# Six chunk-0 loads of a fused RWKV and MLP kernel issued by ScalarE in place of SyncE

## The chip, the core and the metric

The kernel runs on one core of a Trainium2 chip. A core has TensorE (matmuls; it reads SBUF and writes PSUM), VectorE, ScalarE and GpSimd (work on tiles, each taking its own instructions in order) and SyncE, which here does nothing but issue DMAs. ScalarE issues some DMAs as well, between its other instructions. The profile calls the engines PE (and PEld for weight loads), DVE, ACT, POOL and SP; ACTq and SPq are the instruction queues in which an engine issues its DMAs. The metric is the device time of one execution in microseconds, from inputs in DRAM to the output in DRAM.

## The reference

Inputs are r, k and v of shape (4 batches, 8 heads, 768 steps, 48), decays w and bonuses u of shape (8, 48), and an MLP with gain g and weights 384 x 1536 and 1536 x 384, all in float32. A recurrence over the steps is followed by a normalised two-layer MLP with a residual:

```python
for t in range(S):
    kt, vt, rt = (k[:, :, t].copy(), v[:, :, t].copy(), r[:, :, t].copy())
    cur = np.einsum('bhd,bhe->bhde', u[None] * kt, vt)
    y[:, :, t] = np.einsum('bhd,bhde->bhe', rt, state + cur)
    state = w[None, :, :, None] * state + np.einsum('bhd,bhe->bhde', kt, vt)
...
xn = (x - mu) / np.sqrt(var + 1e-06) * g_ln
ch = np.maximum(xn @ w_ch1, 0.0) @ w_ch2
return (x + ch).astype(np.float32)
```

Here x is y with its 8 heads side by side, 384 wide.

## The kernel before

**Tiles.** The 768 steps are cut into 6 chunks of 128. A tile i is chunk i // 4 of batch i % 4, so there are 24 tiles, and tiles 0 to 3 are chunk 0 of the four batches. Within a chunk the recurrence becomes matrix products: r and k are scaled by powers of the decay (steps SR and SK, which write `sc`), transposed (TR on TensorE, copied to SBUF by TCr, TCk or TC), multiplied into a 128 x 128 matrix per head (AT) and masked (AM, AMa, AMb, on VectorE). Y multiplies that with v and adds the state of earlier chunks; S makes the next state and the bonus term, of which ZU and CC take the parts out of PSUM. Q is the product of the transposed r and k for the bonus, CV turns v to bf16, VB multiplies v by the bonus, and X adds it to Y. Then come the MLP's steps: XN (centre), LT and XT (transpose), UP and RL (first layer), DN (second layer), OT (scale and residual), STO (store).

**Pairs in chunk 0.** Batches 0 and 1 share one pair of tiles, and so do 2 and 3. A load of chunk 0 takes 192 KB of one batch to 64 partitions, two neighbouring steps in each; the tile that SK, SR and CV read is one of the two steps over all 128 partitions. So SK0 and SK1 each read what LK0 and LK1 loaded, SR2 and SR3 what LR2 and LR3 loaded, CV2 and CV3 what LV2 and LV3 loaded, and so on. From chunk 1 on a load fills a tile of its own.

**Order.** The order of all work is written out by hand in `PLAN`: each entry is a step's name, its index and a letter for the engine or the PSUM bank. Every engine takes its own entries in that order; between engines there are semaphores alone. The letter s stands for ScalarE, v for VectorE and g for GpSimd. The loads LK, LR and LV (lines 376 to 383) all call `load` (lines 363 to 371), which issues one DMA from SyncE and has no use for the letter, which in the plan is "-". SyncE issues a load as soon as it comes to it, unless the tile's ring slot is still in use or its queue is full. A helper `issuer(e)` (line 206) is used by the small loads at the start and by the stores: it gives ScalarE for s, and SyncE for anything else.

**Around the change.** The plan's entries for SyncE begin with LK1, LV0, LR1, LR0, LK0, LK2, LK3, LV1, LR2, LR3, LV2, LR4, LV3, LV4, LR5, LK4, LK5 and then the three LW1 (768 KB each of the first layer's weights). ScalarE's entries begin with four small loads (WF and three LC), the table load TL, the logarithm LN, and then the exponentials and copies GK0, CP, FK, GR1, GR0, GK1, FR (which overwrites LN's output in place), CV1, TCk0, UGC, TCr0, TCk1, WL, CC0, TCr3, TCk3, TCr2, CC1, CV3, VB0. TensorE's order is WB, CT, dummy matmuls DU, TR0, TR1, DU, AT0, TR3, S0, AT1, DU, TR2, S1, Y1, AT3, AT2, S3, Y0, TR4, and so on up to UP0. GpSimd's entries, after the constants, are SK0, UW, SR3, SR2, Q1, CV2, VB1, SK4, SR4, Q2, SK5. VectorE's are SR1, SR0, SK1, SK3, SK2, CV0, TCr1, Q0 and the masks.

Of the kernel before, what the change touches and what calls it, by code (L numbers as in the profile page):

```python
# [15 lines left out]
K_BY_DMA = [12, 13, 14, 15, 16, 17, 18, 19, 20, 21, 22, 23]  # L16
SLOTS = {'kf': 10, 'rf': 10, 'vf': 11, 'sc': 5, 'vv': 5, 'trs': 5, 'q': 3, 'A': 4, 'cc': 5, 'Z': 6, 'ZS': 2, 'Vb': 4, 'x': 12, 'xn': 6, 'xT': 4, 'hT': 4, 'ot': 4}
PLAN = """
MZ,0,g MI,0,g MM,0,g WF,0,s MW,0,v LC,0,s LC,2,s LC,1,s WB,0,h LK,1,- LV,0,- LR,1,- LR,0,- TL,0,s LN,0,s MP,0,v MQ,0,v LK,0,- GK,0,s SK,0,g CT,0,o
CP,0,s FK,0,s UW,0,g GR,1,s SR,1,v DU,39,h GR,0,s SR,0,v TR,0,- GK,1,s SK,1,v TR,1,o FR,0,s LK,2,- LK,3,- SK,3,v SK,2,v LV,1,- CV,1,s TCk,0,s UGC,0,s  # L20
CV,0,v TCr,1,v TCr,0,s LR,2,- LR,3,- DU,11,p Q,0,v AT,0,- AMa,0,v AMb,0,v SR,3,g TR,3,h TCk,1,s WL,0,s S,0,o CC,0,s ZU,0,v AT,1,- DU,2,a AMb,1,v
TCr,3,s TCk,3,s Q,3,v AMa,1,v SR,2,g TR,2,- TCr,2,s TCk,2,v Q,1,g S,1,h CC,1,s LV,2,- LR,4,- LV,3,- CV,2,g LV,4,- LR,5,- SR,5,v Y,1,h ZU,1,v AT,3,-
AM,3,v VB,1,g X,1,v AT,2,- CV,3,s S,3,- ZU,3,v VB,0,s Y,0,h X,0,v LK,4,- SK,4,g SR,4,g AMb,2,v AMa,2,v XN,1,s TR,4,h TC,4,s CV,4,s SQ,1,s CC,3,v Q,4,v
Q,2,g S,2,h ZU,2,v CC,2,v VB,2,v LT,1,- LK,5,- SK,5,g TR,5,h TC,5,v LW1,0,- SW,1,s SW,0,s Y,3,o XN,0,g LT,0,- XT,0,s XT,1,s SW,2,g VB,3,g Y,2,h X,2,v
X,3,v LW1,1,- SW,3,v SW,5,g Q,5,v S,4,- SW,4,s UP,0,- CC,4,s RL,0,s UP,16,- RL,16,s XN,2,g LT,2,o XT,2,v ZU,4,v LW1,2,- SW,8,s SW,7,g ATP,4,- AM,4,v
# [40 lines left out]
def kernel(  # L66
# [12 lines left out]
    nc = tc.nc  # L79
    P = nc.NUM_PARTITIONS  # L80
    B, H, S, D = r.shape
# [8 lines left out]
    FK = F // P  # L90
# [23 lines left out]
    def ring(name, shape, dtype):  # L114
        n = SLOTS[name]
        tiles = [const.tile(shape, dtype, name=f"{name}{a}") for a in range(n)]
        return lambda i: tiles[i % n]

    def pairs(name, shape, dtype):
        n = SLOTS[name]  # L120
        tiles = [const.tile([P, 2] + shape, dtype, name=f"{name}{a}") for a in range(n // 2)]
        rest = [const.tile([P] + shape, dtype, name=f"{name}_{a}") for a in range(n % 2)]
        return tiles, lambda i: tiles[i % n // 2][:, i % n % 2] if i % n // 2 < len(tiles) else rest[0][:]

    kp, kf = pairs("kf", [H, D], FP32)
    rp, rf = pairs("rf", [H, D], FP32)
    vp, vf = pairs("vf", [H, D], FP32)
# [78 lines left out]
    def issuer(e):  # L206
        return nc.scalar if e == "s" else nc.sync

    def chunk_src(t, i):
        c, b = divmod(i, B)  # L210
        return t[b, :, c * L : (c + 1) * L, :].rearrange("h t d -> t h d")
# [148 lines left out]
    def both(t, i):  # L360
        return t[i // 2][:].rearrange("p a h d -> p (a h d)").rearrange("p (h j d) -> p h j d", h=H, j=2)

    def load(ring, pair, src, i):
        if i >= B:
            nc.sync.dma_start(out=ring(i), in_=chunk_src(src, i))  # L365
        else:
            b0 = i % 2 * DP
            nc.sync.dma_start(  # L368
                out=pair[i // 2][b0 : b0 + DP].rearrange("p a h d -> p (a h d)").rearrange("p (h x) -> p h x", h=H),
                in_=src[i, :, :L, :].rearrange("h (p j) d -> p h (j d)", j=2),  # L370
            )
# [2 lines left out]
        return ring(i) if i >= B else both(pair, i)[:, :, i % 2]  # L374

    def LK(i, e):
        load(kf, kp, k, i)

    def LR(i, e):
        load(rf, rp, r, i)  # L380

    def LV(i, e):
        load(vf, vp, v, i)

    def SK(i, e):
        times(e, sck(i)[:, :, :D], rows_of(kf, kp, i), Fk[:] if i >= B else F0[i % 2][1][:])
# [316 lines left out]
    def STO(i, e):  # L703
# [11 lines left out]
        MQ=MQ, MZ=MZ, GK=GK, GR=GR,  # L715
        WF=WF, WB=WB, LC=LC, CT=CT, CP=CP, LT2=LT2, TKR=TKR, DU=DU, MW=MW, TL=TL, MI=MI, MM=MM, MP=MP, LN=LN, FK=FK_, FR=FR_, UGC=UGC,
        UW=UW, WL=WL, LW1=LW1, SW=SW, LW2=LW2, CW=CW, LK=LK, LR=LR, LV=LV, SK=SK, SR=SR, CV=CV, TR=TR, TCr=TCr,
        TCk=TCk, TC=TC, Q=Q, AT=AT, ATP=ATP, AMa=AMa, AMb=AMb, AM=AM, S=S_, CC=CC, ZU=ZU, ZD=ZD, VB=VB, Y=Y, X=X,
        SQ=SQ, XN=XN, RS=RS, LT=LT, LTD=LTD, TKD=TKD, TRD=TRD, XT=XT, UP=UP, RL=RL, DN=DN, OT=OT, STO=STO, DA=DA, DB=DB, OA=OA, OB=OB, SA=SA, SB=SB,
    )  # L720
    for step in PLAN.split():
        name, i, e = step.split(",")
# [31 lines left out]
```

## Time and profile before

| what | us |
|---|---|
| median of three runs | 153.09 |
| the three runs | 151.73 to 153.7 |
| the profiled execution | 153.01 |
| its span, first to last instruction | 151.2 |
| busy in the span: TensorE matmuls | 139.2 |
| VectorE | 113.4 |
| GpSimd | 88.2 |
| ScalarE | 86.4 |

The span is the part of an execution that the trace shows; the 1.8 us around it belong to the run's time. A row of a timeline gives the start of a group of like instructions, how long the group lasted, the engine, the line of the kernel, the operation and the tiles (written <- read); the bracket at its end is the time that the engine stood idle ahead of it and what ended that. Many steps share the line of a helper (204 for products, 199 and 201 for copies), so the tiles tell them apart: `sc<-rf` is an SR, `sc<-kf` an SK, `vv<-vf` a CV, `Vb<-vf,cc` a VB. DMA-issuing instructions are not counted as busy time. A load's landing is the time from its issue until its data is there.

### The profile page before, as it was taken

How to read it: one execution, taken by the hardware profiler on the slowest of the kernel's cores; microseconds unless marked ns; L12 is line 12 of the kernel's file. 1: busy time of each engine (PE TensorE's matmuls, PEld its weight loads, DVE VectorE, ACT ScalarE, POOL GpSimd, SP SyncE). 2: the span in 40 equal slices, each digit the busy share in tenths (PEclk: the TensorE clock that was granted, in tenths of full speed). 3: DMA queues.
4: the chain of work that ended last, by engine and by line, in shares of the span. 5: the costliest groups of instructions: out<-in, count | busy, mean ns of one | idle time of the engine just before them, and what ended most of it. 6: DMA issues, size and time to landing. Idle time of an engine off the chain costs nothing.

```text
span 151.2 us, 4597 instructions
## 1 busy us (share of the span) xinstructions
PE 139.2 (92%) x1843; PEld 112.2 (74%) x1843; DVE 113.4 (75%) x224; ACT 86.4 (57%) x228; POOL 88.2 (58%) x115
## 2 busy tenths in 40 slices
PE   3398959999999999998999979999999999999992
PEld 1247748999977779885679749977778966979781
DVE  3087997599978899699798897887974566866352
ACT  1667967586965526686328354688873640543710
POOL 7055699782999595787375682639615139741000
PEclk9999995699999999999999999999999999999999
DMA  2999999799988997999889999999999994850112
GB/s 62 237 225 195 179 336 353 142 181 327 377 167 177 216 181 152 201 225 182 169 124 237 203 168 188 206 174 243 175 255 215 251 153 90 231 154 5 56 52 104
DMA packets 92868, 28.61 MB, mean 189 GB/s; under 512 B 88364, under 2 KB 91056, under 8 KB 92848
## 3 DMA queue, kind: packets, MB, share of 16 engines
q1 hardware_dynamic: 91952, 27.24, 85.6%
q10 hardware_dynamic: 896, 1.09, 2.0%
q8 instruction: 14, 0.23, 0.6%
q14 instruction: 6, 0.05, 0.1%
HBM read 18.88 MB, written 4.72 MB: 156 GB/s over the span
## 4 chain that ended last, share of the span: by engine, by line
PE 65%; DMA 10%; SPq 10%; DVE 7%; issue 3%; POOL 2%; ACT 2%; DVEq 0%; ACTq 0%
PE hp L610 19%; PE o L640 12%; PE s L640 11%; DMA vf<-in_v_dram 7%; SPq L368 6%; PE o L610 4%; DMA kf<-in_k_dram 3%; PE at L435 3%; DVE A L445 3%; PE s L610 3%; SPq L365 2%; PE at L399 1%; PE hp L485 1%; PE hp L538 1%; PE hp L516 1%
## 5 line engine op out<-in xcount | busy, mean ns | idle before, releaser
L610 PEld LDWEIGHTS <-w_sb 128*128 128x128 bf16 x612 | 49.8, 115 | 3.1 <-issue 0.6
L610 PE MATMUL hp<-xT,w_sb 128*128 128x128 bf16 (+1 forms) x456 | 42.0, 242 | 0.4 <-DVE x L545 0.4
L640 PEld LDWEIGHTS <-hT 128*128 128x128 bf16 x276 | 24.9, 98 | 15.0 <-ACT hT L626 1.5
L626 ACT ACTIVATE hT<-hp 128x512 bf16<-128x512 f32 x40 | 23.5, 594 | 18.7 <-PE hp L610 17.0
L445 DVE TENSOR_TENSOR A<-at,mask 128x1024 bf16<-128x1024 f32 (+1 forms) x27 | 29.2, 1097 | 3.3 <-PE at L435 3.3
L640 PE MATMUL o<-w_sb,hT 128*128 128x384 bf16 x144 | 27.4, 326 | 1.2 <-ACT hT L626 1.0
L640 PE MATMUL s<-w_sb,hT 128*128 128x384 bf16 x132 | 25.4, 326 | 0.0
L204 POOL TENSOR_TENSOR q<-trs 128x512 bf16<-128x512 bf16 x11 | 13.1, 1202 | 10.9 <-DMA trs<-sc 4.1
L204 POOL TENSOR_TENSOR Vb<-vf,cc 128x384 f32<-128x384 f32 x14 | 11.9, 852 | 9.0 <-issue 4.2
L204 POOL TENSOR_TENSOR sc<-rf,Fr 128x384 bf16<-128x384 f32 x13 | 13.6, 1045 | 5.1 <-DMA rf<-in_r_dram 5.1
L204 POOL TENSOR_TENSOR sc<-kf,Fk 128x384 bf16<-128x384 f32 x14 | 14.6, 1048 | 2.7 <-DMA kf<-in_k_dram 2.1
L552 ACT ACTIVATE sqj<-x,sm 128x384 bf16<-128x384 f32 x24 | 14.7, 611 | 0.1
L545 DVE SCALAR_TENSOR_TENSOR x<-hp,Vb 128x384 f32<-128x384 f32 x20 | 10.9, 551 | 4.9 <-PE hp L538 2.6
L628 DVE TENSOR_SCALAR hT<-hp 128x512 bf16<-128x512 f32 x12 | 8.3, 688 | 7.8 <-PE hp L610 7.7
L199 ACT CAST vv<-vf 128x384 bf16<-128x384 f32 x11 | 5.5, 508 | 11.0 <-DMA vf<-in_v_dram 11.0
L560 POOL TENSOR_SCALAR xn<-x,sm 128x384 bf16<-128x384 f32 x12 | 7.3, 611 | 7.5 <-DVE x L545 7.3
L204 POOL TENSOR_TENSOR Z<-ZS,WLZ 128x384 bf16<-128x384 f32 x9 | 9.0, 1013 | 1.2 <-DVE ZS L498 1.2
L201 POOL CAST vv<-vf 128x384 bf16<-128x384 f32 x10 | 6.0, 603 | 5.3 <-DMA vf<-in_v_dram 4.8
L610 PE MATMUL o<-xT,w_sb 128*128 128x256 bf16 (+1 forms) x84 | 9.1, 250 | 0.0
L698 DVE SCALAR_TENSOR_TENSOR ot<-o,rs,x 128x384 f32<-128x384 f32 x12 | 7.3, 611 | 1.7 <-PE o L640 1.1
L399 PEld LDWEIGHTS <-sc 128*128 128x128 bf16 x96 | 6.7, 108 | 2.1 <-POOL sc L204 1.8
L698 DVE SCALAR_TENSOR_TENSOR ot<-s,rs,x 128x384 f32<-128x384 f32 x11 | 6.7, 611 | 1.5 <-PE s L640 1.5
(138 smaller groups left out, 236.9 us busy)
## 6 DMA issues: line engine op xcount, KB each, us to landing
kf<-in_k_dram SPq DMA_DIRECT2D x24, 192.0 KB, 3.9
vf<-in_v_dram SPq DMA_DIRECT2D x24, 192.0 KB, 4.1
rf<-in_r_dram SPq DMA_DIRECT2D x24, 192.0 KB, 4.1
w_f<-in_moe_w_ch_dram SPq DMA_DIRECT2D x6, 768.0 KB, 6.1
out_dram<-ot SPq DMA_DIRECT2D x18, 192.0 KB, 3.4
out_dram<-ot ACTq DMA_DIRECT2D x5, 192.0 KB, 1.9
trs<-sc SPq DMA_TRANSPOSE x12, 3.4
xT<-xn SPq DMA_TRANSPOSE x9, 3.8
```

The costliest lines, as they stand in the source:

```text
L204: engines[e].tensor_tensor(out=out, in0=in0, in1=in1, op=ALU.mult)
L368: nc.sync.dma_start(out=pair[i // 2][b0 : b0 + DP].rearrange("p a h d -> p (a h d)").rearrange("p (h x) -> p h x", h=H), in_=src[i, :, :L, ...
L399: nc.tensor.transpose(out=t[:, a * HP + q, :], in_=flat[:, q, :], identity=ident[:])
L445: nc.vector.tensor_tensor(out=AA(i)[:, a:b].rearrange("p e q t -> p (e q) t"), in0=psum["at", i][:, a:b].rearrange("p e q t -> p (e q) t") ...
L545: nc.vector.scalar_tensor_tensor(out=xx(i)[:], in0=psum["y", i][:, :C], scalar=1.0, in1=Vb(i)[:], op0=ALU.mult, op1=ALU.add, accum_out=sm[ ...
L552: nc.scalar.activation(out=sqj[:], in_=xx(i)[:], func=ACT.Square, bias=sm[i][:], scale=-float(C), accum_out=sq[g][:, j : j + 1])
L560: engines[e].tensor_scalar(out=xn(i), in0=xx(i)[:], scalar1=-float(C), scalar2=sm[i][:], op0=ALU.mult, op1=ALU.add)
L610: nc.tensor.matmul(out=t[:, a * gw : (a + 1) * gw].rearrange("p (j t) -> p j t", j=size), lhsT=w1_sb[n][kc][:, fb::FB], rhs=xT(g)[:, :size ...
L626: nc.scalar.activation(out=o, in_=s, func=ACT.Relu)
L628: nc.vector.tensor_relu(out=o, in_=s)
L640: nc.tensor.matmul(out=psum["o", i][:, :C], lhsT=hT(g)[:, fk, j * P : (j + 1) * P], rhs=w2_sb[d][:, a, :], start=(seen == 0 and a == 0), s ...
L698: nc.vector.scalar_tensor_tensor(out=ot(i), in0=psum["o", i][:, :C], scalar=rs[g][:, j : j + 1], in1=xx(i)[:], op0=ALU.mult, op1=ALU.add,)
```

## The change

In chunk 0, the loads of k, r and v of the second batch (index 1) and of the fourth (index 3) get the letter s in the plan, at the places at which they stood. The load functions hand the letter on, and `load` uses `issuer(e)`. The six DMAs are the same; ScalarE issues them, each between the ScalarE entries around it: LK1 and LR1 between the small loads and TL, LK3 and LV1 between FR and CV1, LR3 between TCr0 and TCk1, LV3 between CC1 and CV3. Loads with "-" stay with SyncE, and all other entries stay as they were.

```diff
-MZ,0,g MI,0,g MM,0,g WF,0,s MW,0,v LC,0,s LC,2,s LC,1,s WB,0,h LK,1,- LV,0,- LR,1,- LR,0,- TL,0,s LN,0,s ...
+MZ,0,g MI,0,g MM,0,g WF,0,s MW,0,v LC,0,s LC,2,s LC,1,s WB,0,h LK,1,s LV,0,- LR,1,s LR,0,- TL,0,s LN,0,s ...
-... FR,0,s LK,2,- LK,3,- SK,3,v SK,2,v LV,1,- CV,1,s TCk,0,s UGC,0,s
+... FR,0,s LK,2,- LK,3,s SK,3,v SK,2,v LV,1,s CV,1,s TCk,0,s UGC,0,s
-CV,0,v TCr,1,v TCr,0,s LR,2,- LR,3,- DU,11,p Q,0,v ... TCk,1,s ...
+CV,0,v TCr,1,v TCr,0,s LR,2,- LR,3,s DU,11,p Q,0,v ... TCk,1,s ...
-... S,1,h CC,1,s LV,2,- LR,4,- LV,3,- CV,2,g LV,4,- LR,5,- ...
+... S,1,h CC,1,s LV,2,- LR,4,- LV,3,s CV,2,g LV,4,- LR,5,- ...

-    def load(ring, pair, src, i):
+    def load(ring, pair, src, i, e):
         if i >= B:
-            nc.sync.dma_start(out=ring(i), in_=chunk_src(src, i))
+            issuer(e).dma_start(out=ring(i), in_=chunk_src(src, i))
         else:
             b0 = i % 2 * DP
-            nc.sync.dma_start(
+            issuer(e).dma_start(
...
     def LK(i, e):
-        load(kf, kp, k, i)
+        load(kf, kp, k, i, e)
```

LR and LV hand on their letter in the same way.

More of the change, by code (lines that the diff above doesn't have):

```diff
@@ L18 @@
 PLAN = """
[L19 to L22, printed above, removed]
+MZ,0,g MI,0,g MM,0,g WF,0,s MW,0,v LC,0,s LC,2,s LC,1,s WB,0,h LK,1,s LV,0,- LR,1,s LR,0,- TL,0,s LN,0,s MP,0,v MQ,0,v LK,0,- GK,0,s SK,0,g CT,0,o
+CP,0,s FK,0,s UW,0,g GR,1,s SR,1,v DU,39,h GR,0,s SR,0,v TR,0,- GK,1,s SK,1,v TR,1,o FR,0,s LK,2,- LK,3,s SK,3,v SK,2,v LV,1,s CV,1,s TCk,0,s UGC,0,s
+CV,0,v TCr,1,v TCr,0,s LR,2,- LR,3,s DU,11,p Q,0,v AT,0,- AMa,0,v AMb,0,v SR,3,g TR,3,h TCk,1,s WL,0,s S,0,o CC,0,s ZU,0,v AT,1,- DU,2,a AMb,1,v
+TCr,3,s TCk,3,s Q,3,v AMa,1,v SR,2,g TR,2,- TCr,2,s TCk,2,v Q,1,g S,1,h CC,1,s LV,2,- LR,4,- LV,3,s CV,2,g LV,4,- LR,5,- SR,5,v Y,1,h ZU,1,v AT,3,-
 AM,3,v VB,1,g X,1,v AT,2,- CV,3,s S,3,- ZU,3,v VB,0,s Y,0,h X,0,v LK,4,- SK,4,g SR,4,g AMb,2,v AMa,2,v XN,1,s TR,4,h TC,4,s CV,4,s SQ,1,s CC,3,v Q,4,v
@@ L376, in LK @@
     def LK(i, e):
-        load(kf, kp, k, i)
+        load(kf, kp, k, i, e)
     def LR(i, e):
-        load(rf, rp, r, i)
+        load(rf, rp, r, i, e)
     def LV(i, e):
-        load(vf, vp, v, i)
+        load(vf, vp, v, i, e)
     def SK(i, e):
```

## The prediction

> **What bounds the kernel now.** I read the page first, then the stretches of the span, the chain of waits from its start, the timelines of SyncE, ScalarE, GpSimd and TensorE up to 30 us, and last the landing times of single loads. In the stretches, the columns are the busy time of each engine, the granted TensorE clock, the share of the DMA engines and what they moved.
>
> ```profile
> span 151.2 us, 4597 instructions
> 6.00:8.00 2.00, 1.62 (x5) 0.93 (x6) 0.00 (x0) 1.01 (x3) 0.00 (x0) 1.00 1.27 218
> 20.00:22.00 2.00, 0.62 (x8) 0.45 (x8) 2.00 (x7) 0.95 (x2) 2.00 (x2) 1.00 1.03 378
> 20.00:30.00 10.00, 8.50 (x138) 7.40 (x140) 7.29 (x21) 6.30 (x13) 8.72 (x11) 0.66 0.95 286
> 30.00:40.00 10.00, 10.00 (x202) 9.63 (x199) 9.40 (x19) 8.19 (x21) 6.64 (x7) 1.00 0.99 289
> 100.00:110.00 10.00, 9.81 (x119) 7.06 (x118) 8.29 (x17) 8.21 (x26) 7.48 (x8) 1.00 1.13 225
> ```
>
> There are two regimes. From 30 us TensorE is busy 10.00 of 10.00 us, and from 100 to 110 still 9.81, so it is the bound and has next to no gaps that could soak up a late start. Ahead of 30 us the kernel is a chain of dependent steps: TensorE works 0.62 of the 2 us from 20 to 22, and its clock is 0.66 in the mean from 20 to 30. A delay in the early chain is therefore paid in full at the end. The DMA engines are full early too (share 1.27 from 6 to 8 us, at 218 GB/s, by which one load of 192 KB takes 197 / 218 = 0.90 us).
>
> SyncE issues the loads one after another (start, duration, queue, line, tile):
>
> ```profile
> 0.73 0.77 SPq L368 DMA_DIRECT2D kf<-in_k_dram  x1
> 2.23 1.52 SPq L368 DMA_DIRECT2D rf<-in_r_dram  x2
> 3.79 1.99 SPq L368 DMA_DIRECT2D kf<-in_k_dram  x3
> 5.83 0.83 SPq L368 DMA_DIRECT2D vf<-in_v_dram  x1
> 6.70 1.75 SPq L368 DMA_DIRECT2D rf<-in_r_dram  x2
> 10.21 1.57 SPq L368 DMA_DIRECT2D vf<-in_v_dram  x1
> 14.08 4.84 DMA kf<-in_k_dram
> 18.99 0.67 POOL sc L204
> 27.62 2.16 PE hp L610 x24
> ```
>
> By the order of the plan, LK1 is at 0.73, LR1 is the first of the two at 2.23, LK3 is the last of the three at 3.79, LV1 is at 5.83, LR3 the second of the two at 6.70, LV3 at 10.21: all six are on their way by then, however late their users come. The last three rows are from the chain of waits: a K load of chunk 1 (4.84 us) releases GpSimd at 18.99, and from 27.62 on the chain is TensorE.
>
> **The six issues on ScalarE.** ScalarE takes its steps in order. Its timeline around the new places:
>
> ```profile
> 2.58 0.64 ACTq L222 DMA_DIRECT2D rows<-in_u_dram  x1
> 3.25 1.28 ACT L240 ACT_TABLE_LOAD   x1 [3.25 <-DVE eps L290]
> 6.99 0.17 ACT L199 COPY cols<-o 128x11 f32<-128x11 f32 x1 [1.30 <-PE o L229]
> 9.21 0.61 ACT L315 ACTIVATE Fr<-Fr,pow_i 128x384 f32<-128x384 f32 x1
> 11.19 0.51 ACT L199 CAST vv<-vf 128x384 bf16<-128x384 f32 x1 [1.36 <-DMA vf<-in_v_dram]
> 12.70 0.58 ACT L199 COPY trs<-at 128x512 bf16<-128x512 bf16 x1
> 17.10 0.17 ACT L199 COPY cc<-hp 128x8 f32<-128x8 f32 x1
> 17.29 0.51 ACT L199 CAST vv<-vf 128x384 bf16<-128x384 f32 x1
> 94.70 0.60 ACT L626 ACTIVATE hT<-hp 128x512 bf16<-128x512 f32 x1 [0.88 <-PE hp L610]
> 94.71 0.39 ACTq L712 DMA_DIRECT2D out_dram<-ot  x1
> 88.62 0.60 DVE L698 SCALAR_TENSOR_TENSOR ot<-s,rs,x 128x384 f32<-128x384 f32 x1
> ```
>
> The three rows at the foot say when a DMA on ScalarE goes out. The row at 88.62 is VectorE's last output product ahead of the store, so the store's data was there no later than 88.62 + 0.60, yet it was issued at 94.71, 0.01 us after the activation ahead of it had stopped waiting 0.88 us for TensorE. So an issue does not pass a waiting step, but it needn't wait for that step's end (94.70 + 0.60).
>
> The Trainium skill (Perfetto Trace Analysis, section "DVE / Act Engine Instruction") has the sequencer push an activation into a wait queue and then fetch the next instruction. Taken alone, that would let all six loads leave early, in about 153 us; the 94.71 row disagrees.
>
> *LK1 and LR1* come behind the small loads, ahead of the table load. Two issues at about 0.65 us (the 0.64 of the row at 2.58) move the table load from 3.25 to about 4.6, and the work behind it by 1.4 us; the copy at 6.99 had idled 1.30 us for TensorE, so only 0.15 us is left at the exponential at 9.21. LR1 leaves at about 4.0, not at 2.23. Its users:
>
> ```profile
> 8.20 1.06 DVE L204 TENSOR_TENSOR sc<-rf,F 128x384 bf16<-128x384 f32 x2 [3.79 <-ACT F L276]
> 10.69 0.53 PE L300 MATMUL hp<-warm 128*128 128x128 bf16 x3
> ```
>
> At 5.3 us from issue to landing (the 5.5 below is its nearest row when the queue is full) LR1 lands at 9.3, and VectorE's pair SR1, SR0 starts 1.1 us late, ending at 10.4. That lies beside the dummy matmuls, which keep TensorE until 10.69 + 0.53 = 11.2. I cost it at nothing; if LR1 landed after about 10 us the cover would be gone, at 1 us for each us.
>
> *LK3 and LV1* stand behind the exponential at 9.21: LK3 goes at 9.4, not about 5.1, LV1 at 10.05, not 5.83. Behind LV1 stands the cast CV1 at 11.19, which needs that load, and behind the cast the copies of the transposed tiles, the last at 12.70. For the landings I have these rows (the median from issue to landing of the loads issued in a short stretch, in us):
>
> ```profile
> kf<-in_k_dram SPq DMA_DIRECT2D x1, 192.0 KB, 3.2
> rf<-in_r_dram SPq DMA_DIRECT2D x2, 192.0 KB, 5.5
> rf<-in_r_dram SPq DMA_DIRECT2D x1, 192.0 KB, 5.9
> kf<-in_k_dram SPq DMA_DIRECT2D x1, 192.0 KB, 9.2
> rf<-in_r_dram SPq DMA_DIRECT2D x1, 192.0 KB, 4.2
> ```
>
> They were issued at 0.73 (empty engines), about 7.4, 9.34, about 19.9 (behind the weights) and 28.98. What a load on ScalarE's own queue takes while SyncE's is full, no row shows: 3.2 us is the low end, 5.9 the high end, 9.2 the end beside the weights. For LV1, second of two, I take 5.5, as issued nearest in time. It lands at 10.05 + 5.5 = 15.55 and CV1 starts 4.4 us late. VectorE is stuck as well: SK3 needs LK3, and CV0 reads the tile that LV0 and LV1 share.
>
> *LR3* stands behind the copy at 12.70, 1.5 us after the cast of which 0.5 was idling: 15.55 + 1.0 = 16.55. It used to be issued at 7.4. Landing 4.84 us, as the K load of 14.08, gives 21.4. Who waits for it:
>
> ```profile
> 13.06 2.14 POOL L204 TENSOR_TENSOR sc<-rf,F 128x384 bf16<-128x384 f32 x2 [1.88 <-DMA rf<-in_r_dram]
> 16.26 0.50 POOL L201 CAST vv<-vf 128x384 bf16<-128x384 f32 x1
> 17.35 0.83 POOL L204 TENSOR_TENSOR Vb<-vf,cc 128x384 f32<-128x384 f32 x1 [0.59 <-ACT cc L199]
> 18.99 1.00 POOL L204 TENSOR_TENSOR sc<-kf,Fk 128x384 bf16<-128x384 f32 x1 [0.81 <-DMA kf<-in_k_dram]
> 19.95 1.00 POOL L204 TENSOR_TENSOR sc<-rf,Fr 128x384 bf16<-128x384 f32 x1
> 14.12 0.62 PE L399 MATMUL hp<-ident,sc 128*128 128x128 bf16 x8 [0.37 <-POOL sc L204]
> 21.00 0.62 PE L399 MATMUL hp<-ident,sc 128*128 128x128 bf16 x8 [1.18 <-POOL sc L204]
> ```
>
> GpSimd's SR3 starts at 21.4 in place of 13.06, 8.3 us late. TensorE's TR3 (14.12) is queued ahead of S0, AT1, TR2 and S1, and ScalarE's copy CC1 at 17.10 follows S1, so all of it moves by 8.3 us; CC1 starts at 25.4.
>
> *LV3* stands behind CC1, is issued at 25.45 in place of 10.21, and with 4.2 us (the row of 28.98) lands at 29.65. Both casts CV2 (GpSimd, 16.26) and CV3 (ScalarE, 17.29) read the tile of which it is half. GpSimd now runs CV2 at 29.65, VB1 (0.83) at 30.15, SK4 at 31.0, SR4 at 31.9, without its old waits of 0.59 and 0.81. TR4, behind SR4, starts at 32.95 in place of 21.00.
>
> **The SyncE side.** Its queue loses six issues and every later load is issued up to some 5 us sooner: LK4, LK5 and the weights no longer are what ends last. That gain, the 0.81 us, is already in the sum, because TR4 is placed by GpSimd without that wait. SyncE has no new wait. The DMA engines move the same bytes.
>
> **The sum.** +4.4 by CV1, +3.9 more by SR3, +3.65 more by TR4, together 32.95 - 21.00 = 11.95 us. From TR4 on GpSimd, VectorE and TensorE follow in the same order. The low clock (0.66 from 20 to 30) comes after the idle stretch of TensorE, which both kernels have there, so I count no change for it. The profiled execution took 153.01 us (151.2 of span and 1.8 around it; the median of the runs is 153.09): 153.0 + 12.0 = 165.0 us.
>
> By the Trainium skill (DMA: Bandwidth & Descriptors, section "Queues, rings and completion order") each DMA engine takes turns between the queues. ScalarE's loads would then overtake SyncE's backlog: an estimate is 3.2 + 0.9 = 4.1 us for a single load, LV1 at 15.3, and about 163.9 us in all. No row here has two full queues.
>
> **The rivals.** *A smaller delay:* the new queue is served at once, each load 3.2 us. LV1 is 2.3 us earlier, LR3 1.6 more and LV3 1.0 more: 165.0 - 4.9 = 160.1; if LR3 is also issued as soon as CV1 has stopped waiting (16.55 becomes 15.7) 159.3. For it: ScalarE's queue is empty. Against it: the DMA share is at or above 1.0 throughout.
>
> *A larger one:* LR3 and LV3, issued when the weights are moving, take 5.9 to 9.2 us. 5.9 for all three adds 0.4 + 1.1 + 1.7 = 3.2, so 168.2; 9.2 for one of them adds some 4 more, 172. Against it: the weights were sent sooner, and LV3 may come after them.
>
> *Faster:* SyncE's serial issues are what bound the start. The six removed took some 5.5 us (0.77 + 0.76 + 0.66 + 0.83 + 0.87 + 1.57, means where a row holds several), so LK4 leaves at 8.6 and lands at 13.4 instead of 18.9. The idle 1.18 us of TensorE at 21.00 goes, and with it, if it caused the clock of 0.66, up to 10 x 0.34 = 3.4 us: 153.0 - 1.2 - 3.4 = 148.4. It decides only if LV1, LR3 and LV3 land by 11.2, 13.1 and 16.3, that is, if ScalarE's issues pass its waiting copies. The 94.71 row speaks against that. *No change* needs the same passing, with the first loads late by as much as SyncE's are early: about 153.
>
> **How the numbers follow.** Forecast (161 to 168) 0.68; smaller delay (156 to 161) 0.16; larger 0.08; no change 0.05; faster 0.03. The likeliest is 165.0. The range 159 to 169 goes from the low end of all three landings to just above their high end and leaves out some 0.17. About 2% is what a measurement of this kernel can tell from no change, 150.0 to 156.2: faster 0.03, within 0.05, slower 0.92.
>
> **What would show it.** ScalarE's table load near 4.6; its issues of LK3 and LV1 at 9.4 to 10.1, of LR3 just after CV1 (15 to 17), of LV3 behind CC1 (24 to 26). GpSimd idle for rf until about 21, then for vf until about 29.5; TensorE idle ahead of TR3; the chain's first UP group near 39.5 in place of 27.62. The forecast is wrong if ScalarE issues LR3 ahead of CV1's start, if its loads land within 3 us or need over 6, or if TensorE after 40 us has gaps that the late start fills.

## The result, and the profile after

| kernel | median, us | to the kernel before | 95% interval |
|---|---|---|---|
| before | 153.39 | | |
| changed | 170.19 | 1.110 | 1.098 to 1.123 |

The change costs 16.8 us, 11%. The direction and the path were as forecast; 165.0 was too low, and the time lies above the range. The profiled execution of the changed kernel took 168.47 us with a span of 166.7, so 15.5 us more span than before; the other three runs took 169.68 to 170.92. The medians here and below are over all runs; the ratios and their intervals leave out slow runs, those more than 1.5% above the fastest of the same kernel.

ScalarE's timeline of the changed kernel (start, duration, queue or engine, line, tiles; the bracket is the idle time ahead and what ended it):

```profile
4.69 1.28 ACT L240 ACT_TABLE_LOAD   x1 [4.69 <-DVE pow L258]
9.45 0.60 ACTq L368 DMA_DIRECT2D kf<-in_k_dram  x1
10.09 0.65 ACTq L368 DMA_DIRECT2D vf<-in_v_dram  x1
16.19 0.51 ACT L199 CAST vv<-vf 128x384 bf16<-128x384 f32 x1 [6.14 <-DMA kf<-in_k_dram]
16.30 0.67 ACTq L368 DMA_DIRECT2D rf<-in_r_dram  x1
30.87 0.17 ACT L199 COPY cc<-hp 128x8 f32<-128x8 f32 x1 [0.25 <-PE hp L485]
30.88 0.60 ACTq L368 DMA_DIRECT2D vf<-in_v_dram  x1
33.91 0.51 ACT L199 CAST vv<-vf 128x384 bf16<-128x384 f32 x1 [2.88 <-DMA vf<-in_v_dram]
```

Each late load goes out as soon as the last step ahead of it that had to wait has started: LK3 0.01 us after FR (9.44), LV1 right behind it at 10.09, LR3 0.11 us after the start of CV1 at 16.19, LV3 0.01 us after CC1 at 30.87. LR3 did not wait for the copies TCk0 and TCr0, which stand between CV1 and it in the plan and started at 16.61 and 17.20. The bracket at 16.19 names a K load, but what CV1 reads is v: by the trace, LV1 took 6.0 us to land, which is 16.1. GpSimd and TensorE wait for them in turn:

```profile
25.11 1.95 POOL L204 TENSOR_TENSOR sc<-rf,F 128x384 bf16<-128x384 f32 x2 [14.90 <-DMA rf<-in_r_dram]
33.95 0.50 POOL L201 CAST vv<-vf 128x384 bf16<-128x384 f32 x1 [5.78 <-DMA vf<-in_v_dram]
34.41 0.83 POOL L204 TENSOR_TENSOR Vb<-vf,cc 128x384 f32<-128x384 f32 x1
26.16 1.03 PE L399 MATMUL hp<-ident,sc 128*128 128x128 bf16 x8 [7.70 <-POOL sc L204]
37.21 1.03 PE L399 MATMUL hp<-ident,sc 128*128 128x128 bf16 x8 [0.94 <-POOL sc L204]
```

GpSimd stood 14.90 us idle for LR3 and 5.78 us for LV3. The last two rows are TR3 and TR4; TR4 starts 16.2 us later than the 21.00 of before, and that is the whole loss, to 0.7 us. The stretches (TensorE, its weight loads, VectorE, ScalarE, GpSimd, clock, DMA share, GB/s) show every engine at zero from 20 to 24 us, while LR3 is on its way, clock 0.50 when work goes on, and later TensorE full as before:

```profile
20.00:22.00 2.00, 0.00 (x0) 0.00 (x0) 0.00 (x0) 0.00 (x0) 0.00 (x0) 0.50 1.07 382
22.00:24.00 2.00, 0.00 (x0) 0.00 (x0) 0.00 (x0) 0.00 (x0) 0.00 (x0) 0.50 1.10 313
28.00:30.00 2.00, 1.94 (x31) 1.60 (x30) 1.73 (x4) 1.14 (x3) 0.16 (x1) 0.50 1.18 207
30.00:32.00 2.00, 2.00 (x62) 1.85 (x62) 1.70 (x4) 0.75 (x2) 0.00 (x0) 0.50 0.55 104
140.00:150.00 10.00, 10.00 (x131) 7.43 (x130) 8.02 (x15) 3.66 (x11) 7.17 (x9) 1.00 0.53 131
```

At 382 GB/s from 20 to 22 us the DMA engines were far from idle: they moved the weights. The chain of waits names the longest step, and SyncE's timeline says what had been sent just ahead of LR3:

```profile
16.30 8.65 DMA rf<-in_r_dram
```

```profile
14.22 2.28 SPq L336 DMA_DIRECT2D w_f<-in_moe_w_ch_dram  x3
16.54 0.81 SPq L365 DMA_DIRECT2D rf<-in_r_dram  x1
27.03 1.61 SPq L365 DMA_DIRECT2D vf<-in_v_dram  x2
41.61 5.78 SPq L353 DMA_DIRECT2D w_f<-in_moe_w_ch_dram  x3
```

The three weight loads, 2.36 MB, left from 14.22 on; LR3 followed at 16.30 on the other queue. SyncE then ran through its loads by 28.6 and waited until 41.61 for the weights' buffers, so when LV3 went out at 30.88 the DMA engines had little left to do (share 0.55 from 30 to 32 us), and it took 3.0 us.

### The profile page after: what moved, and what is told of

The parts are those of the page before. It is cut to its first block, busy times and chain, and to the rows that moved or that the text cites. A ratio compares the mean times of both kernels' runs of the same rounds, so it can differ in the third digit from the quotient of the medians.

```text
span 166.7 us, 4594 instructions
## 1 busy us (share of the span) xinstructions
PE 142.2 (85%) x1843; PEld 114.7 (69%) x1843; DVE 113.5 (68%) x224; ACT 86.0 (52%) x228; POOL 87.3 (52%) x115
## 4 chain that ended last, share of the span: by engine, by line
PE 64%; DMA 12%; DVE 9%; issue 6%; POOL 4%; ACTq 2%; SPq 1%; ACT 0%; POOLq 0%; DVEq 0%
PE hp L610 18%; PE o L640 12%; PE s L640 11%; DMA rf<-in_r_dram 8%; PE o L610 4%; DVE A L445 3%; PE s L610 3%; DMA kf<-in_k_dram 3%; PE at L435 3%; POOL sc L204 2%; PE hp L538 2%; PE hp L516 2%; PE at L399 1%; POOL q L204 1%; PE hp L485 1%
## 5 line engine op out<-in xcount | busy, mean ns | idle before, releaser
L640 PE MATMUL s<-w_sb,hT 128*128 128x384 bf16 x132 | 25.4, 326 | 0.1
L399 PE MATMUL hp<-ident,sc 128*128 128x128 bf16 x32 | 3.7, 288 | 8.6 <-POOL sc L204 8.6
L204 POOL TENSOR_TENSOR sc<-rf,F 128x384 bf16<-128x384 f32 x2 | 1.9, 994 | 14.9 <-DMA rf<-in_r_dram 14.9
```

The source lines that it names most:

```text
L204: engines[e].tensor_tensor(out=out, in0=in0, in1=in1, op=ALU.mult)
L399: nc.tensor.transpose(out=t[:, a * HP + q, :], in_=flat[:, q, :], identity=ident[:])
L640: nc.tensor.matmul(out=psum["o", i][:, :C], lhsT=hT(g)[:, fk, j * P : (j + 1) * P], rhs=w2_sb[d][:, a, :], start=(seen == 0 and a == 0), s ...
```

## The experiments

Line numbers in these kernels are lower by 6 (the plan is wrapped otherwise); "after" in the table is the changed kernel. The lines with "-" in a diff are the changed kernel's, and in the last one those of the kernel before. "Weights behind LV3", "LR3 alone" and "LV3 alone" are on record as unclear against before, though their whole intervals lie above 1.02; what is read from them rests on their traces as well.

| kernel | median, us | to before, 95% interval |
|---|---|---|
| LR3 back on SyncE | 165.14 | 1.071 to 1.087 |
| weights later | 171.20 | 1.113 to 1.131 |
| weights behind LV3 | 167.08 | 1.086 to 1.102 |
| LK1, LR1 alone | 152.80 | 0.995 to 1.004 |
| LK3, LV1 alone | 159.32 | 1.032 to 1.049 |
| LR3 alone | 158.37 | 1.027 to 1.043 |
| LV3 alone | 162.18 | 1.054 to 1.067 |
| six, issued early | 153.71 | 0.990 to 1.003 |
| three, issued early | 153.24 | 0.996 to 1.006 |
| after, with dummies | 169.44 | 1.085 to 1.112 |
| before, with dummies | 151.05 | 0.980 to 0.999 |
| three early, with dummies | 152.74 | 0.995 to 1.004 |

**LR3 back on SyncE.**

```diff
-TCr,0,s LR,2,- LR,3,s
+TCr,0,s LR,2,- LR,3,-
```

> Only LR3 goes back to SyncE; the other five loads stay on ScalarE. If the late kernel is a chain of waits on ScalarE's loads, of which LR3's landing (8.8 us after its issue at 16.30) is the largest link, then GpSimd has SR3 and SR2 done early, TensorE goes on from AT0 at about 18 straight to TR3, CC1 starts at about 21.5 in place of 30.87, and LV3 is issued there: the time falls by 7 to 10 us, to 160 to 163. If LR3 was covered by something else that is late anyway (the masks, Q1), the time falls by less than 4, to above 166.

165.14 us, 5.0 less than the changed kernel and between the two expectations. SR3 started at 10.27, so LR3 was off the path, but CC1 came at 24.12 and not at 21.5: CV1 was at 17.21 in this run, and then the same chain went on, from 20 us on at a clock of 0.50. LV3, sent at 24.13 while the queues were full, took 5.9 us. So LR3 is one link of several, and taking it out lengthens the next.

**Weights later.** SyncE's order with all six loads on ScalarE: eight loads of later tiles ahead of the weights.

```diff
-LW1,0,- LW1,1,- LW1,2,- ... LR,8,- LK,7,- LR,7,- LK,6,- LV,5,- LR,6,- LV,7,- LV,6,-
+LR,8,- LK,7,- LR,7,- LK,6,- LV,5,- LR,6,- LV,7,- LV,6,- LW1,0,- LW1,1,- LW1,2,-
```

> All six loads on ScalarE as in the changed kernel, but SyncE issues eight loads of 192 KB for later tiles (LR8 to LV6) ahead of the three weight loads LW1 and not behind them. Theory A, that LR3 landed late because the weights were ahead of it in the DMA engines: LR3's landing falls from 8.8 to 4.5 to 6 us, and LV3, which is then the one issued beside the weights, rises from 3.0 to 5 us or more; the time is 166 to 171 as the two add up. Theory B, that ScalarE's queue is served slowly whatever SyncE sends: LR3 still takes 8 us or more and LV3 stays near 3.

ScalarE's and SyncE's issues and GpSimd's first user of each load, from the timeline, and the stretches around LV3:

```profile
16.83 0.61 ACTq L362 DMA_DIRECT2D rf<-in_r_dram  x1
21.42 1.95 POOL L198 TENSOR_TENSOR sc<-rf,F 128x384 bf16<-128x384 f32 x2 [12.45 <-DMA rf<-in_r_dram]
23.37 2.04 SPq L330 DMA_DIRECT2D w_f<-in_moe_w_ch_dram  x3
27.19 0.60 ACTq L362 DMA_DIRECT2D vf<-in_v_dram  x1
35.77 0.50 POOL L195 CAST vv<-vf 128x384 bf16<-128x384 f32 x1 [11.29 <-DMA vf<-in_v_dram]
```

```profile
26.00:28.00 2.00, 2.00 (x53) 1.84 (x55) 1.70 (x5) 0.75 (x2) 0.00 (x0) 0.50 1.02 344
28.00:30.00 2.00, 1.19 (x42) 1.04 (x33) 1.54 (x2) 0.00 (x0) 0.00 (x0) 0.50 1.04 393
30.00:32.00 2.00, 0.00 (x0) 0.00 (x0) 0.00 (x0) 0.00 (x0) 0.00 (x0) 0.50 1.06 397
32.00:34.00 2.00, 0.00 (x0) 0.00 (x0) 0.00 (x0) 0.00 (x0) 0.00 (x0) 0.50 0.52 114
```

Theory A holds and B falls. LR3, now ahead of the weights, took 4.4 us to land by the chain of waits, and 21.42 - 16.83 = 4.6 from its issue to its user's start; LV3, now behind them, took 35.77 - 27.19 = 8.6. The time, 171.2, did not fall, because one gain paid for the other loss. The stretches show how: from 26 to 32 us the engines moved 2 x (344 + 393 + 397) = 2270 KB, nearly all of it on SyncE's queue, against 2360 KB of weights. LV3's own packets came between 31.1 and 35.3 us.

**Weights behind LV3.** LW1 uses `issuer(e)` too, and ScalarE sends the weights after both late loads.

```diff
-LV,3,s CV,2,g ... LW1,0,- ... LW1,1,- ... LW1,2,-
+LV,3,s LW1,0,s LW1,1,s LW1,2,s CV,2,g ...
```

> All six loads on ScalarE at the places of the changed kernel; the three weight loads LW1 are issued by ScalarE too, right behind LV3, and so behind both late loads. Theory A, that a load waits for the weights issued ahead of it: LR3 lands in 4.5 to 5 us and LV3, with the weights behind it, in 3 to 4.5 us; TR4 starts at 32 to 34 and the time is 164 to 167, about what the prediction's sum gave. If the weights share the engines with a load whatever the order, LV3 takes 6 us or more and the time is 168 or more.

```profile
27.59 0.60 ACTq L362 DMA_DIRECT2D vf<-in_v_dram  x1
28.23 1.71 ACTq L330 DMA_DIRECT2D w_f<-in_moe_w_ch_dram  x3
30.91 0.50 POOL L195 CAST vv<-vf 128x384 bf16<-128x384 f32 x1 [6.03 <-DMA vf<-in_v_dram]
34.17 1.03 PE L393 MATMUL hp<-ident,sc 128*128 128x128 bf16 x8 [0.93 <-POOL sc L198]
```

With 2.36 MB sent right behind it, LV3 still landed in 3.3 us, and LR3 in 4.6 by the chain. What counts is what was sent ahead of a load. TR4 came at 34.17, 3.0 us sooner than in the changed kernel and 1.2 later than forecast: LR3 left 0.5 us late, as LV1 took 6.9 us, the link from SR3 to CC1 took 1.7 us more than forecast, and LV3 gave 0.9 back. The median fell by 3.1, to 167.08, just above what was expected, but its interval (1.086 to 1.102) overlaps that of the changed kernel (1.098 to 1.123), and the profiled execution took 168.29 us, only 0.2 less than that of the changed kernel. The 3.0 us of TR4 were lost again later: at 102.86 us TensorE had idled 2.06 us for ScalarE, which had waited 3.10 us for a V load, and its clock fell to 0.50 from 104 to 106. So the landing is shown; that the gain reaches the end is not.

**The parts alone.** For each, all other letters go back to "-".

LK1 and LR1:

> Only LK1 and LR1 on ScalarE, the other four on SyncE. The prediction cost these two at nothing: 152.5 to 154, with SR1 about 1 us later than 8.20 and TR1 not later than before. Its rival: VectorE's SR1 and what follows move the whole start by over 1 us, 154.5 or more.

152.80 us, the same as before. SR1 started at 9.67 and not 8.20, but TR0 at 10.76, no later than the 11.01 of before, and TR4 only 0.16 us later: the zero of the prediction stands.

LK3 and LV1:

> Only LK3 and LV1 on ScalarE, at their places behind the exponentials; the rest on SyncE. They go out at about 9.2 and 9.9, land at about 14 and 15.5, so CV1 and SK3 start 4 to 5 us late and AT0 too; LR3 and LV3 are on time. By the prediction's term for CV1 (+4.4) the time is 156 to 158.5. If VectorE's queue behind SK3 costs more than ScalarE's behind CV1: above 159. If later slack takes it up: below 155.5.

```profile
10.06 0.70 ACTq L362 DMA_DIRECT2D vf<-in_v_dram  x1
16.51 0.51 ACT L193 CAST vv<-vf 128x384 bf16<-128x384 f32 x1 [6.58 <-DMA vf<-in_v_dram]
```

159.32 us, some 6.4 over the before of its chip (152.89) and in the bracket above 159, but not for the reason given there: the chain runs from LV1 through CV1 and ScalarE's copies to TensorE, without VectorE. CV1 was 5.3 us late. From TR3 (18.71) to CC1 (23.42) it then took 4.7 us and not 3.0, with the clock at 0.50 from 20 us on; TR4 was 6.1 us late.

LR3:

> Only LR3 on ScalarE, at its place behind the copy of r; the rest on SyncE. By the chain theory it is issued at about 11.5 to 12.8, ahead of the weights, lands 5 to 6 us later at 17 to 18.5, and SR3 starts 4 to 5.5 us later than 13.06; the time rises by 3.5 to 6 us, to 156.5 to 159. If the place did not matter (the landing hidden): below 154.5. If ScalarE's queue always takes 8 us or more: above 160.

```profile
11.93 0.71 ACTq L362 DMA_DIRECT2D rf<-in_r_dram  x1
17.52 1.94 POOL L198 TENSOR_TENSOR sc<-rf,F 128x384 bf16<-128x384 f32 x2 [6.53 <-DMA rf<-in_r_dram]
```

158.37 us, +5.0: sent ahead of the weights, it had a user after 5.6 us. SR3 was 4.5 us late and TR4 5.95; the clock was 0.50 from 16 us on.

LV3:

> Only LV3 on ScalarE, behind CC1; the rest on SyncE. It is issued at about 17.2, within a us of the weights that SyncE sends from about 15.5 on. Theory A (behind the weights): it lands 7 to 9 us later, at 24 to 26, CV2 moves from 16.26 to there, and the time rises by 5.5 to 9 us, to 158.5 to 162. If the weights ahead did not hold it up: landing 3 to 5 us, time 155 to 157.

```profile
15.04 3.07 SPq L330 DMA_DIRECT2D w_f<-in_moe_w_ch_dram  x3
16.89 0.71 ACTq L362 DMA_DIRECT2D vf<-in_v_dram  x1
26.11 0.50 POOL L195 CAST vv<-vf 128x384 bf16<-128x384 f32 x1 [10.15 <-DMA vf<-in_v_dram]
```

162.18 us, +8.8: sent 1.85 us after the first of the weights, it took 9.2 us. The three parts add up to 6.4 + 5.0 + 8.8 = 20.2 us, more than the 16.8 together. In the whole change only one load meets the weights: LR3 and LV3 took 8.65 + 3.0 us there, and 5.6 + 9.2 alone, which is 3.1 of the 3.4 us.

**The same engine, early places.** All six on ScalarE, with LK3, LV1, LR3 and LV3 right behind the table load:

```diff
-TL,0,s LN,0,s
+TL,0,s LK,3,s LV,1,s LR,3,s LV,3,s LN,0,s
```

> All six loads on ScalarE, but LK3, LV1, LR3 and LV3 stand right behind the table load and not behind the exponentials, CV1 and CC1. Theory A, that the place behind waiting steps is what costs: all six are issued by about 8 us, and the time is 153 to 156 (the logarithm and the exponentials start some 3 us later, of which 1.3 was idle). Theory B, that loads on ScalarE's queue are slow in themselves: 158 or more, with landings of 6 us and more at ScalarE's loads.

And LV1, LR3 behind the table load, LV3 behind GK0, the other three on SyncE:

> LV1 and LR3 issued by ScalarE right behind the table load and LV3 right behind the first exponential, where ScalarE's engine runs the load or idles; LK1, LR1 and LK3 stay on SyncE. No issue stands behind a wait. By theory A nothing is late: 151.5 to 153.5, with LK4 up to 1 us sooner than 18.99. If the shorter queue of SyncE were worth what the faster rival gave it, below 150.

153.71 and 153.24 us, neither told apart from before. With no issue behind a wait the loss is gone, though ScalarE still issues six loads; that settles place against queue. The faster rival found no support: neither run was measurably faster than before, and with three loads moved SK4, the user of LK4, started at 19.24 and not before 18.99, though it no longer waited for its load.

**The clock.** Dummy matmuls in the changed kernel, 24 wide ones ahead of TR3 and 5 ahead of S3:

```diff
-TR,3,h
+DU,96,p TR,3,h
-S,3,-
+DU,20,p S,3,-
```

> The changed kernel, all six loads late, with dummy matmuls added on TensorE: 24 wide ones (128x512) ahead of TR3 and 5 ahead of S3, in stretches in which TensorE idled 7.70 and 1.62 us. If the low clock lengthened the chain between the late loads, the granted clock is 1.00 in most of 22 to 36 us, the stretch from SR3's start to CC1's start falls from 5.76 us to 4.0 to 4.6, and the time falls by 1.5 to 4 us, to 166 to 169. If the low clock there costs nothing: within 1 us of 170. If the dummies run over the arrival of LR3: above 171.

From the timeline, SR3 and the issue behind CC1; from the stretches, the clock in the column ahead of the DMA share:

```profile
24.73 1.95 POOL L198 TENSOR_TENSOR sc<-rf,F 128x384 bf16<-128x384 f32 x2 [15.22 <-DMA rf<-in_r_dram]
29.22 0.60 ACTq L362 DMA_DIRECT2D vf<-in_v_dram  x1
```

```profile
24.00:26.00 2.00, 0.81 (x7) 0.32 (x6) 0.00 (x0) 0.00 (x0) 1.27 (x2) 1.00 1.38 212
28.00:30.00 2.00, 2.00 (x54) 1.84 (x55) 2.00 (x6) 0.85 (x3) 0.00 (x0) 0.50 0.91 179
```

SR3 to CC1 took 4.5 us, not 5.76, with the clock at 1.00 or close to it (0.95 from 26 to 28) up to about 28 us: the low clock lengthened that link by 1.3. The median fell only from 170.19 to 169.44, and the intervals overlap, so the gain at the end is not shown. From 28 us the clock was 0.50 again, in spite of the second group.

The same idea in the kernel before, 4 wide dummies ahead of TR4:

```diff
-TR,4,h
+DU,16,o TR,4,h
```

> The kernel before, with 4 wide dummy matmuls ahead of TR4, where TensorE idled 1.18 us. If that gap set off the low clock from 22 to 29 us, and TensorE was the bound there, the time falls by 1 to 3 us, to 150 to 152. If the clock depends on more than that gap, or GpSimd and VectorE bound that stretch: within 1 us of 153.

```profile
20.00:22.00 2.00, 1.41 (x12) 0.63 (x10) 2.00 (x7) 0.89 (x2) 2.00 (x3) 1.00 1.03 392
24.00:26.00 2.00, 2.00 (x65) 1.64 (x59) 2.00 (x5) 2.00 (x5) 2.00 (x3) 1.00 1.13 349
```

The clock stayed at 1.00, and the time was 151.05 us, 1.0% below before with an interval that ends at 0.999. With the three early loads added:

> LV1, LR3 and LV3 issued early by ScalarE, as in the run with three early loads, together with the 4 dummy matmuls ahead of TR4. If a shorter SyncE queue is worth something once the low clock is out of the way: below 150.5. If it is worth nothing, as DMA engines and GpSimd bound the start: 150.5 to 152, as with the dummies alone (151.05). If the clock still drops: 153.

152.74 us, no different from before, though the profiled execution again had clock 1.00 throughout its span. So the dummies' 1% may be real, but the runs do not settle it, and nothing here beats the kernel before by a clear margin.

## Why the prediction was wrong

The steps as predicted, and as the changed kernel's trace has them, in us:

| step | predicted | measured |
|---|---|---|
| table load starts | 4.6 | 4.69 |
| LV1 issued, landing takes | 10.05, 5.5 | 10.09, 6.0 |
| CV1 starts | 15.55 | 16.19 |
| LR3 issued, landing takes | 16.55, 4.84 | 16.30, 8.65 |
| SR3 starts | 21.4 | 25.11 |
| CC1 starts | 25.4 | 30.87 |
| LV3 issued, landing takes | 25.45, 4.2 | 30.88, 3.0 |
| CV2 starts | 29.65 | 33.95 |
| TR4 starts | 32.95 | 37.21 |

**The chain was right.** Which three loads carry the loss, and who waits for each, came out as written. LR3's issue came out on time by luck: LV1 landed 0.5 us later than forecast, and LR3 then left 0.1 and not 1.0 us after CV1's start, as it did not wait for the copy of r. LK1 and LR1 cost nothing, as forecast, by their own run, and TensorE could not soak up the delay: of 16.2 us at TR4, 15.5 are in the span.

**The step that failed is the landing of LR3, "Landing 4.84 us, as the K load of 14.08".** It took 8.65, 3.8 more, by the chain. That K load left SyncE ahead of the weights; LR3 now left behind them. The prediction had the cause in hand and turned it round: it put the weights' earlier issue down as a reason against the larger rival ("the weights were sent sooner"), where sooner, 14.22 and not 16.43, meant ahead of LR3. The two runs that shift the weights settle that the cause is their place ahead: LR3 took 4.4 and 4.6 us when it went ahead of them, and LV3 8.6 us behind them and 3.3 ahead. The larger rival, at 0.08, came nearest, with one load beside the weights; but it did not have the next term either.

**A second term was left out.** From SR3 to CC1 it took 5.76 us and not 4.0 (before: 13.06 to 17.10), 1.7 more. "I count no change" for the clock was wrong for this link: TR3 and what follows ran at clock 0.50, where the kernel before had 1.00, and the dummies took 1.3 us of it away. LV3's 3.0 us instead of 4.2 gave 1.2 back. There the smaller rival had the landing nearly right (3.2); the argument against it, a DMA share at or above 1.0 throughout, was misread, as the prediction's own rows have 0.95 and 0.99, and from 18 to 20 us it was 0.76 before the change.

The sum of the table: SR3 +3.7, SR3 to CC1 +1.7, LV3 -1.2, and 37.21 - 32.95 = 4.26. The profiled execution was then 168.47 and not 165.0, with 0.7 taken back after TR4; the median is 1.7 above it, a spread between runs that no trace here explains.

**The two rules.** That a DMA on ScalarE does not pass a waiting step was read from one row and is confirmed at LR3 and LV3, whose issues came 0.11 and 0.01 us after the start of CV1 and CC1. LR3's issue did pass the copies ahead of it that waited for nothing but ScalarE itself.

By the Trainium skill (DMA: Bandwidth & Descriptors, section "Queues, rings and completion order"), each DMA engine takes turns between the queues' rings, by which ScalarE's load should overtake SyncE's backlog in an estimated 4.1 us. Behind the weights it did not: 8.6 us and more with nothing else on its own queue. The packets show where the time went. The pages list the queue q10 (packets, MB, share of the DMA engines) as follows, before and then changed:

```profile
q10 hardware_dynamic: 896, 1.09, 2.0%
q10 hardware_dynamic: 4064, 2.27, 4.9%
```

It has 3168 packets more, 528 for each of the six loads, and SyncE's queue q1 has 3168 fewer; so q10 is ScalarE's. The next table has, in us after the issue, when a load's first packet moved, and when it had landed or its user started:

| load | sent ahead of it | first packet | landed |
|---|---|---|---|
| LR3, changed kernel | the weights | 4.3 | 8.65 |
| LV3, weights later | the weights | 3.9 | 8.6 |
| LV3 alone | the weights | 4.1 | 9.2 |
| LR3, weights later | loads of 192 KB | 1.8 | 4.4 |
| LR3, weights behind LV3 | loads of 192 KB | 1.7 | 4.6 |
| LV3, weights behind LV3 | next to nothing | 1.4 | 3.3 |
| LV3, changed kernel | next to nothing | 1.4 | 3.0 |

Once LR3's packets moved, the queues did take turns: from 21.4 to 23.5 us ScalarE's moved 325 packets and SyncE's 321, with 0.12 and 0.57 MB. In that the trace agrees with the page's rule. But for the first 4.2 us no packet of LR3 moved, while SyncE's queue moved 1.44 MB; the estimate had no such wait. What holds back the first packet, no run here tells.

## What to carry to other kernels

Moving a DMA's issue to a computing engine puts it behind every wait of that engine; in a place with no wait ahead the move was free, and behind a wait it cost the wait plus a full landing. Before pricing a load's landing, list what will have been sent ahead of it on all queues after the change, large transfers first: a shorter queue sends those sooner, and they can then stand ahead of the load that is on the path. A chain that idles TensorE also pays for the lower clock in its own matmuls.

## What the runs showed of the hardware

A 192 KB load on ScalarE's queue, with nothing else waiting on that queue, took 3.0 to 3.3 us with little ahead of it, even with 2.36 MB sent just behind it, 4.4 to 5.9 us among SyncE's other loads of 192 KB, and 8.6 to 9.2 us with 2.36 MB sent by SyncE up to 4 us ahead of it. LV1, with LK3 just ahead on the same queue, took 6.0 to 6.9. Two queues took turns packet by packet, but the first packet of a load behind the weights came 3.9 to 4.3 us after its issue, and 1.4 to 2.1 us where no weights were ahead. And 4 dummy matmuls of 1.0 us together, in one gap of 1.18 us, kept the granted clock at 1.00 where it had been 0.66 for 10 us.
